# Token routing with a reordered chain to the gather, one-hots built in one operation, and first-layer matmuls of the first expert placed between the count groups of the second round

## The chip, the cores and the metric

The kernel runs on one core of a Trainium2 chip. The metric is the device time of one execution in microseconds (us). An execution that the hardware profiler recorded comes with it: its trace holds each instruction of each engine with start and duration.

## The reference

Three layers follow one another. Sink-and-window attention gives 1536 tokens of 512 values. A greedy mixture of eight experts routes them: all 1536 x 8 scores are taken from the highest down, and a token goes to the expert of the score if the token is still free and the expert has fewer than 192 tokens. A second mixture weights all eight experts by a Sinkhorn iteration.

```
for idx in order:                      # scores from the highest down
    tok, e = idx // E, idx % E
    if assigned[tok] >= 0 or counts[e] >= cap:   # cap = N // E = 192
        continue
    assigned[tok] = e
    counts[e] += 1
for e in range(E):
    mask = assigned == e
    out[mask] = maximum(x[mask] @ w1[e], 0) @ w2[e]
```

The change lies in the greedy mixture.

## The kernel before

The greedy assignment is done in eight rounds (r = 0 to 7, called rounds one to eight here). In each round every free token proposes to its best expert that is left; for each proposal the kernel counts how many better ones its expert has, finds the expert whose 192nd token has the highest score, closes that expert, and gathers its 192 tokens as two tiles of 96. The tokens lie as 12 columns of 128 (n = 12); from round five on they are compacted to 6 columns.

One round goes as follows, by the names in the code.

- `propose`: val and the scores L give prop and the score m of each proposal (DVE). PE turns each column of m into a row over all partitions (tile bc, in two PSUM buffers of four columns), ScalarE copies the rows to `row`.
- `count`: for each column c DVE compares the row with m (tiles gt and g; L607, L608, L610), into GB = 4 buffers. The compare over the columns behind c (L610) reads the whole row. PE multiplies these tiles with prop into cnt: 13 matmuls of eight columns for each c, taken in six groups of two columns (26 matmuls, L616). Round one's counts are made within the attention.
- `route`: from cnt DVE forms sel, red and fin; PE sums red over the partitions (tile sm); the highest threshold names the expert (eh); ft holds each chosen token's slot.
- `place_tokens`: DVE builds one-hots oh of the slots (L667, one operation for each column) and ch, PE multiplies them (L674, the slot product), and DVE gets the token numbers, `at` and, as integers, `ixs`. The gather (POOL, L716) reads ixs. After ixs the expert's number EIX is written, on which SyncE's weight loads wait (`load_w`, four loads of 1 MB). In round one the first of these loads is issued earlier, and the three others by ScalarE's queue, after the last row copy of the next proposal.
- `leave`: the chosen tokens and the closed expert are struck out of val.
- `turn_tokens`: PE transposes the gathered tokens (L752), ScalarE copies them to xe.
- `moe1`: 32 matmuls of the first layer (L768, tile mm from xe and the weights wf, relu to hT) and 32 of the second (L779), each of 192 columns in fp32, two rows in the trace. The transposes of the next expert's tokens stand in the middle of the second layer. Then come two products with the second gate (L790).

The scheduler lays out one order for each engine. The routing has a high priority, and `issue_after` pins single instructions behind others; the matmuls of `moe1` fill what PE has left. Each engine then runs its order strictly in sequence, so an instruction that waits holds up all behind it on that engine. The weights share a pool of WB = 6 buffers of 1 MB: round two's first two loads find two free ones. The gathered tokens (xg), xe and row have one buffer each.

Of the kernel before, what the change touches and what calls it, by code (L numbers as in the profile page):

```python
# [8 lines left out]
F32 = mybir.dt.float32  # L9
# [11 lines left out]
def kernel(  # L21
# [494 lines left out]
    def routing_and_moe1():  # L516
# [55 lines left out]
        def propose():  # L572
# [11 lines left out]
            for c0 in range(0, n, 4):  # L584
                pb = ps.tile([P, 4, P], F32, name="bc", bufs=2)
                c1 = min(n, c0 + 4)
# [6 lines left out]
        def count(n, m, prop, row):  # L593
# [3 lines left out]
            turned = st.pop("turned", None)  # L597
            with nullcontext() if turned is None else tc.issue_after(turned):
                nc.tensor.matmul(cnt.rearrange("p c e -> p (c e)"), zb, zb[:, :n * E], start=True, stop=False,
                                 skip_group_check=True)  # L600
            for c0 in range(0, n, GC):
# [12 lines left out]
                for cc, a, b in reversed(blocks):  # L614
                    with nullcontext() if first is None else tc.issue_after(first.ins):
# [5 lines left out]
        def route(r):  # L621
# [11 lines left out]
            nc.vector.tensor_reduce(red, sel.rearrange("p a c e -> p a e c"), axis=AX.X, op=OP.add)  # L633
# [6 lines left out]
            nc.vector.scalar_tensor_tensor(fin, cnt, float(CAP) - 0.5, prop, op0=OP.is_lt, op1=OP.mult)  # L640
# [13 lines left out]
        def place_tokens(r, ft, t1, eh, code, n):  # L654
# [11 lines left out]
            for c in range(n):  # L666
                nc.vector.tensor_scalar(ohs[:, c], slots, ft[:, 2, c:c + 1], None, op0=OP.is_equal)  # L667
            ch = gp.tile([P, n, 2, 2], BF, name="ch", bufs=OB)
            nc.vector.tensor_mul(ch[:, :, 1], code, ft[:, 1].unsqueeze(2).to_broadcast([P, n, 2]))
            nc.vector.tensor_sub(ch[:, :, 0], code, ch[:, :, 1])  # L670
            first = None
            for c in reversed(range(n)):
                with nullcontext() if first is None else tc.issue_after(first.ins):
                    mm = nc.tensor.matmul(sm[:HC, 0:4], ohs[:, c], ch[:, c].rearrange("p h a -> p (h a)"),  # L674
                                          start=(c == n - 1), stop=(c == 0), skip_group_check=True)
                first = first or mm
# [11 lines left out]
        def leave(ft, eh, n):  # L688

            val = st["val"]  # L690
            nc.vector.tensor_scalar(ft[:, 3], ft[:, 0], 0.5, None, op0=OP.is_gt)
            nc.vector.scalar_tensor_tensor(val, eh.unsqueeze(1).to_broadcast([P, n, E]), -100.0, val, op0=OP.mult,
                                           op1=OP.add)
# [47 lines left out]
        XE = {}  # L741
# [15 lines left out]

        def moe1(r):


            w1, w2 = W.pop(r)
            xe = XE.pop(r)
            hT = mp.tile([P, KF, CAP], F32, name="hT", bufs=1)
            for j0 in range(0, KF, 2):
                ph = pm.tile([P, 2, CAP], F32, name="mm", tag="mm", bufs=3)
# [246 lines left out]
```

## Time and profile before

| | |
|---|---|
| median of 3 runs | 1388.39 us (1387.87 to 1389.94) |
| profiled execution | 1387.89 us, its span 1386.2 us |
| PE busy | 1349.7 us, 97% |
| DVE, ScalarE, POOL busy | 811.0, 458.2, 443.3 us |
| granted PE clock, mean | 0.989 |

Busy times are shares of the span, which is the profiled execution without 1.7 us around it. The granted clock is a share of 2.4 GHz; 0.50 is 1.2 GHz. PE's matmuls overlap, so that the time from the start of one to the start of the next is what one costs. An engine's idle time costs nothing where another engine sets the end.

### The profile page before, as it was taken

Reading aid. Unit: us, or ns where it says so; the run is one execution under the profiler, and the core shown is the slowest. Engines: PE = TensorE matmul, PEld = TensorE weight load, DVE = VectorE, ACT = ScalarE, POOL = GpSimd, SP = SyncE. Lnnn points to the kernel's source line nnn. Section 1 sums busy time; section 2 is a strip of 40 time slices with the busy share of each in tenths; the row PEclk is TensorE's granted clock in tenths of the full one; section 3 lists DMA queues with packets and bytes.
Section 4 is the critical chain, followed back from the end, with each engine's and each line's share of the span. In section 5 each row is a group of like instructions: output and inputs, shape, how many; then the busy total and the mean of one; then the engine's idle time right before and its main releaser. Section 6 shows DMA issues by size and latency. Waiting matters only on the chain.

```text
span 1386.2 us, 20957 instructions
## 1 busy us (share of the span) xinstructions
PE 1349.7 (97%) x8195; PEld 1213.9 (88%) x8195; DVE 811.0 (59%) x1921; ACT 458.2 (33%) x975; POOL 443.3 (32%) x612
## 2 busy tenths in 40 slices
PE   7998699999999999999999999999999999999998
PEld 5767599999988998989999998989998998989987
DVE  6777787850458555555555555555555555555554
ACT  6774121221443333333323333333323333333321
POOL 1247010110543333344333333344333333344203
PEclk9999699999999999999999999999999999999999
DMA  7421345477110001011000011011000001011002
GB/s 161 108 62 40 134 167 203 166 185 254 52 31 31 31 31 46 31 34 43 31 31 31 31 32 45 31 36 41 31 31 31 31 33 44 31 38 39 1 1 91
DMA packets 87227, 87.39 MB, mean 63 GB/s; under 512 B 43864, under 2 KB 60248, under 8 KB 87128
## 3 DMA queue, kind: packets, MB, share of 16 engines
q1 hardware_dynamic: 82056, 73.45, 17.1%
q0 software_dynamic: 2944, 9.44, 2.0%
q10 hardware_dynamic: 2128, 3.16, 0.7%
q8 instruction: 64, 1.05, 0.3%
q14 instruction: 35, 0.29, 0.1%
HBM read 79.75 MB, written 6.30 MB: 62 GB/s over the span
## 4 chain that ended last, share of the span: by engine, by line
PE 92%; DVE 4%; ACT 2%; issue 1%; POOL 1%; DMA 0%; POOLq 0%; SPq 0%; DVEq 0%; ACTq 0%
PE pa L927 37%; PE X L870 19%; PE Z L870 9%; PE mm L768 6%; PE mm L779 6%; PE Y L870 5%; PE S L263 2%; ACT pb L276 1%; PE o L322 1%; PE cnt L616 1%; PE PT L312 1%; PE xr L337 1%; DVE pb L266 1%; PE tr L239 1%; POOL out_dram L940 1%
## 5 line engine op out<-in xcount | busy, mean ns | idle before, releaser
L927 PE MATMUL pa<-w,h 128*128 128x512 f32 x2304 | 548.7, 391 | 0.0
L927 PEld LDWEIGHTS pa<-w,h 128*128 128x128 f32 x2304 | 430.3, 188 | 85.2
L938 DVE SCALAR_TENSOR_TENSOR accs<-pa,Pm,accs 128x512 f32<-128x512 f32 x360 | 269.8, 749 | 133.3 <-PE pa L927 130.9
L509 POOL TENSOR_TENSOR w<-r,w 128x256 fp32r<-128x256 f32 x128 | 90.4, 739 | 365.8 <-ACT w L505 365.8
L878 DVE SCALAR_TENSOR_TENSOR h<-sum,h 128x384 fp32r<-128x384 f32 x192 | 136.4, 711 | 58.1 <-ACT h L877 57.9
L489 POOL TENSOR_TENSOR w1l<-r,w1h 128x256 fp32r<-128x256 f32 x96 | 68.6, 743 | 275.1 <-ACT w1h L487 267.1
L877 ACT ACTIVATE h<-sum 128x384 fp32r<-128x384 f32 x192 | 100.4, 523 | 155.9 <-DVE sum L887 155.9
L489 POOL TENSOR_TENSOR w1l<-S,w1h 128x256 fp32r<-128x256 f32 x128 | 102.7, 832 | 0.0
L877 ACT ACTIVATE h<-X 128x384 fp32r<-128x384 f32 x64 | 31.5, 492 | 213.9 <-PE X L870 213.9
L768 PE MATMUL mm<-xe,wf 128*128 128x192 f32 x512 | 96.1, 337 | 0.0
L887 DVE TENSOR_TENSOR sum<-Z,u 128x384 f32<-128x384 f32 x64 | 35.6, 557 | 96.2 <-ACT u L882 96.2
L779 PE MATMUL mm<-hT,wf 128*128 128x192 f32 x512 | 91.5, 331 | 0.0
L887 DVE TENSOR_TENSOR sum<-Y,p 128x384 f32<-128x384 f32 x64 | 35.6, 557 | 88.8 <-PE Y L870 88.7
L768 PEld LDWEIGHTS mm<-xe,wf 128*128 128x128 f32 x512 | 83.4, 193 | 0.1
L779 PEld LDWEIGHTS mm<-hT,wf 128*128 128x128 f32 x512 | 82.6, 190 | 0.5
L716 POOL DMA_INDIRECT xg<-X,ixs x16 | 16.7, 1041 | 168.6 <-PE mm L752 60.6
L878 DVE SCALAR_TENSOR_TENSOR h<-X,h 128x384 fp32r<-128x384 f32 x64 | 35.6, 557 | 53.8 <-ACT h L877 53.8
L882 ACT ACTIVATE p<-X 128x384 f32<-128x384 f32 x64 | 31.4, 491 | 106.8 <-PE X L870 105.0
L882 ACT ACTIVATE u<-X 128x384 f32<-128x384 f32 x64 | 31.5, 492 | 99.3 <-PE X L870 99.3
L505 ACT ACTIVATE w<-r 128x1024 fp32r<-128x1024 f32 x32 | 34.0, 1062 | 89.4 <-PE pa L927 88.2
L276 ACT ACTIVATE pb<-pb,nb 128x264 f32<-128x264 f32 (+1 forms) x96 | 46.3, 488 | 15.6 <-DVE nb L271 15.6
L770 ACT ACTIVATE hT<-mm 128x384 f32<-128x384 f32 x32 | 15.7, 489 | 78.9 <-PE mm L768 78.9
(282 smaller groups left out, 2303.5 us busy)
## 6 DMA issues: line engine op xcount, KB each, us to landing
r<-in_moe_w_dram SPq DMA_DIRECT2D x64, 512.0 KB, 3.4
wf<-in_moe_w_dram SPq DMA_DIRECT2D x29, 1024.0 KB, 7.0
kn<-in_k_dram SPq DMA_DIRECT2D x12, 256.0 KB, 4.1
qn<-in_q_dram SPq DMA_DIRECT2D x12, 256.0 KB, 3.8
vn<-in_v_dram SPq DMA_DIRECT2D x12, 256.0 KB, 3.6
X<-xs POOLq DMA_DIRECT2D x12, 256.0 KB
wf<-in_moe_w_dram ACTq DMA_DIRECT2D x3, 1024.0 KB, 8.8
xg<-X,ixs POOLq DMA_INDIRECT x16
```

What stands on the lines that cost most here:

```text
L276: inorder(nc.scalar.activation(PB[c][:, h, :w], PB[c][:, h, :w], AF.Exp, bias=NB[c][:, 0, h:h + 1], scale=scale, accum_out=NB[c][:, 2, h:h ...
L489: nc.gpsimd.tensor_sub(w1[1][:, o + j], x[:, j], w1[0][:, o + j].bitcast(F32))
L509: nc.gpsimd.tensor_sub(w2[:, 1, f, d], r2[:, f, d], w2[:, 0, f, d].bitcast(F32))
L768: nc.tensor.matmul(ph[:, j - j0, :], w1[j // JH][:, k, j % JH * P:(j % JH + 1) * P], xe[:, k, :], start=(k == 0), stop=(k == KD - 1))
L779: nc.tensor.matmul(py[:, k - k0, :], w2[j // JH][:, j % JH, k * P:(k + 1) * P], hT[:, j, :], start=(j == 0), stop=(j == KF - 1))
L870: nc.tensor.matmul(acc_, w1[a][:, o, k, :], XO[x][t][b][:, k, :], start=(start and n == 0), stop=(stop and n == 3 * KH - 1), skip_group_ch ...
L877: nc.scalar.activation(t[:, 0], x, AF.Relu)
L878: nc.vector.scalar_tensor_tensor(t[:, 1], x, 0.0, t[:, 0].bitcast(F32), op0=OP.max, op1=OP.subtract)
L882: nc.scalar.activation(t, x, AF.Copy)
L887: nc.vector.tensor_add(t, a, b)
L927: nc.tensor.matmul(pa, HT[u, f, h][:, a, j * P:(j + 1) * P], w2[:, b, f, :], start=(n == 0), stop=(n == 3 * FP - 1))
L938: nc.vector.scalar_tensor_tensor(acc[:, c], pa, pe, acc[:, c], op0=OP.mult, op1=OP.add)
```

## The change

- `propose` takes the first four columns of the row in two copies, one of column 0 alone and one of columns 1 to 3.
- `route` moves the two operations on fin behind the reduction red.
- `place_tokens` builds all one-hots in one operation (three operations of four columns in round one), after ch, and multiplies the columns in order.
- `leave` puts its first two operations behind the one-hots.
- `first_layer` is split out of `moe1`. In round one its first 16 matmuls (EARLY = 4 blocks of 128 hidden values, 4 matmuls each, on the first weight half alone) are made ahead of `count`, which pins each of the later count groups of round two behind one of them. `moe1(0)` does the other 16.

```diff
-            for c0 in range(0, n, 4):
+            for c0, c1 in [(0, 1), (1, 4)] + [(x, min(n, x + 4)) for x in range(4, n, 4)]:
                 pb = ps.tile([P, 4, P], F32, name="bc", bufs=2)
-                c1 = min(n, c0 + 4)
...
+            ahead = early if turned is not None else None
...
-                    with nullcontext() if first is None else tc.issue_after(first.ins):
+                    after = first.ins if first else ahead[2 * c0 // GC - 1] if ahead and c0 else None
+                    with nullcontext() if after is None else tc.issue_after(after):
                         mm = nc.tensor.matmul(cnt[:, cc, :], a, b, start=False, stop=(a is blocks[0][1] and c1 == n),
                                               skip_group_check=True)
...
-            nc.vector.tensor_reduce(red, sel.rearrange("p a c e -> p a e c"), axis=AX.X, op=OP.add)
+            summed = nc.vector.tensor_reduce(red, sel.rearrange("p a c e -> p a e c"), axis=AX.X, op=OP.add)
...
-            nc.vector.scalar_tensor_tensor(fin, cnt, float(CAP) - 0.5, prop, op0=OP.is_lt, op1=OP.mult)
+            with tc.issue_after(summed.ins):
+                nc.vector.scalar_tensor_tensor(fin, cnt, float(CAP) - 0.5, prop, op0=OP.is_lt, op1=OP.mult)
...
-            for c in range(n):
-                nc.vector.tensor_scalar(ohs[:, c], slots, ft[:, 2, c:c + 1], None, op0=OP.is_equal)
...
-            nc.vector.tensor_sub(ch[:, :, 0], code, ch[:, :, 1])
-            first = None
-            for c in reversed(range(n)):
-                with nullcontext() if first is None else tc.issue_after(first.ins):
-                    mm = nc.tensor.matmul(sm[:HC, 0:4], ohs[:, c], ch[:, c].rearrange("p h a -> p (h a)"),
-                                          start=(c == n - 1), stop=(c == 0), skip_group_check=True)
-                first = first or mm
+            halves = nc.vector.tensor_sub(ch[:, :, 0], code, ch[:, :, 1])
+            parts = 3 if r == 0 else 1
+            with tc.issue_after(halves.ins):
+                for a in range(parts):
+                    d = slice(a * n // parts, (a + 1) * n // parts)
+                    w = d.stop - d.start
+                    shown = nc.vector.tensor_tensor(ohs[:, d], slots.unsqueeze(1).to_broadcast([P, w, HC]),
+                                                    ft[:, 2, d].unsqueeze(2).to_broadcast([P, w, HC]), op=OP.is_equal)
+            st["slots"] = shown.ins
+            for c in range(n):
+                mm = nc.tensor.matmul(sm[:HC, 0:4], ohs[:, c], ch[:, c].rearrange("p h a -> p (h a)"),
+                                      start=(c == 0), stop=(c == n - 1), skip_group_check=True)
...
-            nc.vector.tensor_scalar(ft[:, 3], ft[:, 0], 0.5, None, op0=OP.is_gt)
-            nc.vector.scalar_tensor_tensor(val, eh.unsqueeze(1).to_broadcast([P, n, E]), -100.0, val, op0=OP.mult,
-                                           op1=OP.add)
+            with tc.issue_after(st["slots"]):
+                nc.vector.tensor_scalar(ft[:, 3], ft[:, 0], 0.5, None, op0=OP.is_gt)
+                nc.vector.scalar_tensor_tensor(val, eh.unsqueeze(1).to_broadcast([P, n, E]), -100.0, val, op0=OP.mult,
+                                               op1=OP.add)
...
+        EARLY = 4
+
+        def first_layer(r, blocks):
+            w1, xe, hT = W[r][0], XE[r], HT[r]
+            made = []
+            for j0 in blocks:
                 ph = pm.tile([P, 2, CAP], F32, name="mm", tag="mm", bufs=3)
                 for j in (j0, j0 + 1):
                     for k in range(KD):
-                        nc.tensor.matmul(ph[:, j - j0, :], w1[j // JH][:, k, j % JH * P:(j % JH + 1) * P], xe[:, k, :],
-                                         start=(k == 0), stop=(k == KD - 1))
+                        made.append(nc.tensor.matmul(ph[:, j - j0, :], w1[j // JH][:, k, j % JH * P:(j % JH + 1) * P], xe[:, k, :],
+                                         start=(k == 0), stop=(k == KD - 1)).ins)
                 nc.scalar.activation(hT[:, j0:j0 + 2, :], ph, AF.Relu)
+            return made
...
+            if r not in HT:
+                HT[r] = mp.tile([P, KF, CAP], F32, name="hT", bufs=1)
+                first_layer(r, range(0, KF, 2))
+            else:
+                first_layer(r, range(EARLY, KF, 2))
...
                     turn_tokens(0)
+                    HT[0] = mp.tile([P, KF, CAP], F32, name="hT", bufs=1)
+                    early = first_layer(0, range(0, EARLY, 2))
```

How the order of the engines moves is shown at three places; where a line number differs between the two kernels, the tiles are the same.

On DVE, in round one, from the masking of fin with the chosen expert to the slot indices (oh are the one-hots, ch the token codes, val the table of what is left), before:

```order
L649 TENSOR_TENSOR fin<-fin,eh 128x96
L692 SCALAR_TENSOR_TENSOR val<-eh,val 128x96
L651 TENSOR_REDUCE ft<-fin 128x12
L662 TENSOR_SCALAR ft<-ft 128x12
L691 TENSOR_SCALAR ft<-ft 128x12
L663 SCALAR_TENSOR_TENSOR ft<-ft 128x12
L669 TENSOR_TENSOR ch<-code,ft 128x12x2
L694 SCALAR_TENSOR_TENSOR val<-ft,val 128x96
L667 TENSOR_SCALAR oh<-slots,ft 128x96 x12
L670 TENSOR_TENSOR ch<-code,ch 128x12x2
L579 TENSOR_REDUCE mx<-val 128x12
L580 SCALAR_TENSOR_TENSOR prop<-val,mx 128x96
```

and the same stretch of DVE with the change:

```order
L653 TENSOR_TENSOR fin<-fin,eh 128x96
L655 TENSOR_REDUCE ft<-fin 128x12
L666 TENSOR_SCALAR ft<-ft 128x12
L667 SCALAR_TENSOR_TENSOR ft<-ft 128x12
L671 TENSOR_TENSOR ch<-code,ft 128x12x2
L672 TENSOR_TENSOR ch<-code,ch 128x12x2
L679 TENSOR_TENSOR oh<-slots,ft 128x384 x3
L700 TENSOR_SCALAR ft<-ft 128x12
L701 SCALAR_TENSOR_TENSOR val<-eh,val 128x96
L687 TENSOR_REDUCE at<-sm 96x2
L703 SCALAR_TENSOR_TENSOR val<-ft,val 128x96
L688 CAST ixs<-at 96x2
```

The updates of val moved behind the one-hots, and the slot indices (at, ixs) ahead of the next proposal's first operations (mx, prop), which follow them now.

On PE, in round two's count, where the first matmuls of the first layer (mm from xe and wf) stand; before, this is the end of the fourth group (after 104 count rows without a break):

```order
L616 LDWEIGHTS gt
L616 MATMUL cnt<-prop,gt 128x8
L768 MATMUL mm<-xe,wf 128x192 x4
L616 LDWEIGHTS g
L616 MATMUL cnt<-prop,g 128x8
```

With the change two of them stand behind each of the first two groups, and eight more are threaded through the third, at whose end it reads:

```order
L619 LDWEIGHTS g
L619 MATMUL cnt<-prop,g 128x8
L776 MATMUL mm<-xe,wf 128x192
L619 LDWEIGHTS gt
L619 MATMUL cnt<-prop,gt 128x8
L776 MATMUL mm<-xe,wf 128x192 x4
```

Up to the end of the sixth group there were 4 and 6 of these matmuls before; now there are 2, 2, 8, 4 and 7 (groups four and five stand together, ahead of the 7). Four follow the sixth group in both.

On PE again, a round's piece later, at the transposes of the tokens that round two gathers (mm from ident and xg); before, they follow two count groups of round three and matmuls of the second layer (mm from hT and wf):

```order
L616 LDWEIGHTS gt
L616 MATMUL cnt<-prop,gt 128x8
L779 MATMUL mm<-hT,wf 128x192 x5
L752 MATMUL mm<-ident,xg_2530 128x96
L752 MATMUL mm<-ident,xg_2532 128x96
```

and with the change they stand behind the slot product (oh) and the row of m (bc), ahead of all count groups of round three:

```order
L683 MATMUL sm<-ch,oh 96x4
L800 MATMUL mm<-hT,wf 128x192 x4
L589 MATMUL bc<-ident,m 128x128 x4
L800 MATMUL mm<-hT,wf 128x192
L589 MATMUL bc<-ident,m 128x128 x8
L800 MATMUL mm<-hT,wf 128x192 x5
L761 MATMUL mm<-ident,xg_2533 128x96
L761 MATMUL mm<-ident,xg_2535 128x96
```

Between the sixth count group and these transposes stood 38 matmuls of the two layers before, and 25 stand there now; both places have 48 of them behind them in all.

## Rows read from the trace of the kernel before

**Rows 1.** Page: the granted PE clock in 40 slices of the span, in tenths.
```profile
PEclk9999699999999999999999999999999999999999
```

**Rows 2.** Windows: busy us of each engine, granted clock, DMA share, GB/s.
```profile
138.00:161.00 23.00, 10.62 (x150) 9.05 (x151) 18.00 (x65) 2.67 (x5) 2.91 (x5) 0.50 0.51 180
...
167.00:195.00 28.00, 28.00 (x343) 27.11 (x341) 23.15 (x75) 5.95 (x12) 1.83 (x2) 1.00 0.45 166
```

**Rows 3.** Timeline of DVE, rounds one and two: start us, us, instruction.
```profile
144.02 1.94 DVE L667 TENSOR_SCALAR oh<-slots,ft 128x96 bf16<-128x96 bf16 x12
...
147.41 0.16 DVE L680 CAST ixs<-at 96x2 int32<-96x2 f32 x1
...
151.60 2.47 DVE L610 TENSOR_SCALAR g<-row,m 128x1408 bf16<-128x1408 f32 x3
...
160.33 0.34 DVE L607 SCALAR_TENSOR_TENSOR gt<-row,m,before 128x128 bf16<-128x128 f32 x1
...
164.56 1.01 DVE L608 TENSOR_SCALAR g<-row,m 128x1536 bf16<-128x1536 f32 x1
...
174.72 0.15 DVE L680 CAST ixs<-at 96x2 int32<-96x2 f32 x1
...
192.10 0.55 DVE L739 TENSOR_TENSOR xB11l<-yT,xB11h 128x384 fp32r<-128x384 f32 x1
```

**Rows 4.** Timeline of PE, rounds one and two.
```profile
146.08 1.04 PE L674 MATMUL sm<-ch,oh 128*96 128x4 bf16 x12 [4.63 <-DVE ch L670]
...
152.87 1.22 PE L752 MATMUL mm<-ident,xg 96*128 96x96 f32 x6 [0.65 <-DMA xg<-X,ixs]
...
167.51 0.17 PE L616 MATMUL cnt<-prop,gt 128*128 128x8 bf16 x1
...
173.79 0.66 PE L674 MATMUL sm<-ch,oh 128*96 128x4 bf16 x12
...
184.20 0.66 PE L752 MATMUL mm<-ident,xg 96*128 96x96 f32 x6
```

**Rows 5.** Chain that ended last, in order of time: start us, us, what.
```profile
160.47 0.86 PE cnt L616 x26
161.32 2.77 PE mm L768 x8
...
169.57 4.33 PE mm L768 x26
...
175.21 0.87 PE bc L589 x8
...
179.96 0.63 PE cnt L616 x26
```

**Rows 6.** Timeline of ScalarE behind the row copies of round one.
```profile
152.49 1.62 ACTq L709 DMA_DIRECT2D wf<-in_moe_w_dram  x3
154.16 0.87 ACT L754 ACTIVATE xe<-mm 128x384 f32<-128x384 f32 x2 [2.63 <-PE mm L752]
```

**Rows 7.** DMA queues (q1 SyncE, q0 POOL): packets, MB; stretches from 152, 179, 180, 182, 211.
```profile
q0 software_dynamic: 30, 0.06, 15.8%
...
q1 hardware_dynamic: 203, 0.42, 107.0%
...
q0 software_dynamic: 63, 0.20, 48.8%
...
q0 software_dynamic: 46, 0.12, 38.5%
...
q0 software_dynamic: 5, 0.00, 1.8%
```

**Rows 8.** Windows: granted clock, third number from the end, around its changes.
```profile
134.50:136.30 1.80, 0.00 (x0) 0.00 (x0) 1.61 (x6) 0.28 (x1) 1.41 (x2) 1.00 0.39 146
137.90:139.00 1.10, 0.75 (x16) 0.56 (x15) 0.47 (x3) 0.00 (x0) 0.89 (x4) 0.50 0.01 4
...
165.00:166.00 1.00, 1.00 (x7) 1.00 (x7) 0.56 (x1) 0.00 (x0) 0.00 (x0) 0.95 0.00 0
```

More of the change, by code (lines that the diff above doesn't have):

```diff
@@ L739, in operands @@
                 nc.vector.tensor_sub(xl, x, xh.bitcast(F32))
-        XE = {}
+        XE, HT = {}, {}
         def turn_tokens(r):
@@ L756, in turn_tokens @@
                 st["turned"] = turned.ins
[L758 to L764, printed above, removed]
+        EARLY = 4
[3 more added lines that the diff above has]
+            for j0 in blocks:
                 ph = pm.tile([P, 2, CAP], F32, name="mm", tag="mm", bufs=3)
@@ L767, in moe1 @@
                     for k in range(KD):
-                        nc.tensor.matmul(ph[:, j - j0, :], w1[j // JH][:, k, j % JH * P:(j % JH + 1) * P], xe[:, k, :],
-                                         start=(k == 0), stop=(k == KD - 1))
+                        made.append(nc.tensor.matmul(ph[:, j - j0, :], w1[j // JH][:, k, j % JH * P:(j % JH + 1) * P], xe[:, k, :],
+                                         start=(k == 0), stop=(k == KD - 1)).ins)
                 nc.scalar.activation(hT[:, j0:j0 + 2, :], ph, AF.Relu)
+            return made
+        def moe1(r):
+            if r not in HT:
[3 more added lines that the diff above has]
+                first_layer(r, range(EARLY, KF, 2))
+            w2 = W.pop(r)[1]
+            del XE[r]
+            hT = HT.pop(r)
             if r % 2 == 0:
```

## The prediction

> **What bounds the kernel now.** The page's clock line comes first: TensorE (PE) has nine tenths of its full speed or more in 39 of 40 slices, and six tenths in the fifth, 139 to 173 us [rows 1]. The windows put that stretch at 138 to 161 us, where round one's routing runs and round two's counting begins: PE works 10.62 of 23 us, at 1.2 GHz (granted 0.50), while VectorE (DVE) works 18. From 167 us PE is full at 2.4 GHz [rows 2]. So the routing is paid for in two currencies: until about 161 us in latency on DVE, after it in PE work alone, as long as PE never waits. What the change is worth is read at one place: how far PE has come when it must next wait for something.
>
> **What the timelines say.** Round one builds its twelve one-hots in 1.94 us, has its slot indices (ixs) at 147.41, and starts the compares over the whole row at 151.60. The compares of columns 8 to 11 begin at 160.33 and the last ends at 164.56 + 1.01 = 165.57 [rows 3]. PE does four count groups before it takes any first-layer matmul (a pass, below; two rows of the trace); the sixth ends at 167.51 + 0.17 = 167.7 with 10 of the 64 matmuls (of expert one's two layers) done. The slot product of round two stands at 173.79, the transposes of its gathered tokens at 184.20 [rows 4]. The chain gives the prices: one pass costs 2.77/4 = 0.69 us at the half clock and 4.33/13 = 0.333 us at the full one, a count group 0.86 or 0.63, a transpose of a column maximum 0.11 [rows 5].
>
> **Round one's chain.** Small operations issue 1.94/12 = 0.16 us apart [rows 3]. Ahead of the one-hots one of the two fin operations goes (0.16; the second stands behind the threshold's maximum instead) and three updates go (0.5). A 128x384 tensor operation takes 0.55 us [rows 3], so three issue in about 1.5 us: 0.4 saved. The slot product takes 1.04 us for twelve columns [rows 4] and now only its last four (0.35) follow the last one-hot: 0.7 saved. ixs come about 1.8 us earlier, at 145.6. The proposal is then all behind them, where two of its operations had lain under the product, so the maxima m gain 1.1 us; the row copies are four instead of three through two PSUM tiles, which costs 0.4 of that: the compares over the whole row start at 150.9, 0.7 earlier. Dropping the reversed order of the slot products and adding the code of early passes costs no instructions; the matmuls are the same ones.
>
> **The gather of round one** lands earlier too, but this isn't what the first passes wait for. ScalarE issues three weight loads in 152.49 to 154.1 and copies xe right behind, at 154.16 [rows 6]. Those loads hang on the last row copy, so xe moves only 0.7 us: the first pass can start at about 154.0.
>
> **Round two's count, by the order.** From 154.0 PE has two passes (155.4), group two (156.25), two passes (157.6) and 17 rows of group three (158.2), all at the half clock. Before, the clock was back at 165.05 [rows 8], 3.9 us after the unbroken stretch that began with the first matmul at 161.2, or 4.6 us after the group of 160.47 [rows 5]. Here the unbroken stretch begins at 154.0; I take the longer of the two, 158.6. The eight passes threaded through group three end at 161.3. The compares of column 8 write the buffer that column 4's rows read until then (four buffers, GB), so they start at 161.3 and not at 159.6, and the four columns take 165.57 - 160.33 = 5.2 us as before: the last compare ends at 166.5. PE meanwhile does four passes, groups four and five and seven passes to 166.9, and the sixth group ends at **167.6**. That is the old time, with 23 matmuls done instead of 10: 13 x 0.333 = **4.3 us** of PE work is in hand.
>
> **Where it goes.** Behind the sixth group the new order has 25 matmuls (8.3 us), the two small products (0.66 at most each, as the slot product [rows 4]) and the twelve transposes of m (1.3) in front of the token transposes: PE is there at 178.4. Before, 38 matmuls and two count groups of the next round stood there. The tokens aren't there yet. Round two's ixs, 7.2 us behind the sixth group before (174.72 + 0.16 [rows 3]), are now 6.6 us behind it (four matmuls, the product, eleven matmuls, the slot product and 0.6 us), at 174.2. From ixs to the last gathered packet passed 8.1 us in that round: the first 1 MB of expert two's weights was taken first, at 0.42 MB in a microsecond and without one gathered packet in 179 to 180; the gather's own packets came in 180 to 183, the last 46 in the last of these microseconds, and none after 183.0 [rows 7]. Both issues hang on the same two DVE operations, ixs and EIX, which still stand together, so the order is the same. In round one, with the queue free, PE had the last tokens at 152.87 [rows 4], 5.3 us after ixs, with the last 30 packets in 152 to 153 [rows 7]; for the step from the last packet to PE I take 0.4 as an estimate from these two. So the tokens can be used at 174.2 + 8.1 + 0.4 = 182.7, and PE **waits 4.3 us**. Counted in states: before, PE began the transposes at 184.20 with 48 matmuls and two groups of round three done; now it begins them at 182.7 with the same 48 and no group, worth 183.96. **0.2 us** is left of the gain. In the old order the transposes stood 0.8 us behind the tokens; that cover is gone.
>
> The Trainium skill, DMA: Bandwidth & Descriptors, section Queues, rings and completion order, says each DMA engine takes turns between the queues that have work. By that the gather would pass the weights at half rate and the wait would be near that of the third case below; this trace doesn't agree: 203 weight packets and no gathered one in 179 to 180 us [rows 7].
>
> **Two later terms.** In round three the new order has PE at the transposes 8.4 us behind ixs (slot product, four matmuls, the m transposes, nine matmuls, a group, three matmuls, a group, one). There the last gathered packets came after 211 us, 9.1 us behind ixs, and with 0.4 more the wait is 1.1; by the 8.5 of round two it is 0.1. I take **0.6**. Round four's transposes stand behind some 27 matmuls and the later ones a whole round behind, so they wait for nothing. And a pause of PE can cost its clock: in 134.5 to 136.3 PE stood still at a granted 1.00, and from 137.9 on it has 0.50 [rows 8]. A wait of 4.3 us is more than twice that pause, so I expect the fall, and the 3.9 to 4.6 us that the return took at half speed cost 1.95 to 2.3 us if it falls at the wait's end, less if earlier: **1.7**, with 0 and 2.3 as ends. The Trainium skill, TensorE: Matmul & The Clock Gate, section HAM oscillation, describes this pattern, a wait for a DMA between bursts that leaves the next burst cold; the row at 137.9 agrees.
>
> **Sum.** The profiled execution took 1387.89 us, 0.5 below the median of 1388.39. 1387.89 - 0.2 + 0.6 + 1.7 = **1390.0 us**, 0.12% above that median: within the 0.2% (2.8 us: 1385.6 to 1391.2) that a measurement of this kernel can tell from no change. The shorter chains of later rounds give nothing, since PE is the bound there and no wait of it was left to shorten.
>
> **Rivals.**
> - *The wait, but no fall of the clock:* 1387.89 - 0.2 + 0.6 = 1388.3. For it speaks that the fall at 137.9 is the only one that the trace shows and came 1.6 us after the pause's end.
> - *The gather isn't held up:* as in round one, 5.3 us behind ixs, at 179.5. The wait is 1.1, too short for a fall, and 1387.89 - 4.3 - 0.1 + 1.1 = 1384.6. Against it stand rounds two and three, whose gathers both came behind the weights [rows 7].
> - *Slower:* the clock comes back as late as it did before, at 165 (in 138 to 161 PE worked 10.62 us and stayed at 0.50 [rows 2]). Then the eight passes in group three take 5.5 us, group three ends at 164.1, column 8's compares wait for it, the sixth group ends at 170.4, and all behind it moves: 1392.8. It decides against "no change" if the clock is back after 161. Against it, the stretch from 154.0 on has no hole.
> - *The passes don't move:* excluded, the order of PE has them there.
>
> **Chances.** The forecast (wait and fall) 0.50, running from 1388.8 to 1392; no fall 0.22; gather not held up 0.13; late clock 0.15. Faster is the third case and a little of unknown cause, 0.14; slower the fourth and the upper end of the first, 0.28; same 0.58. The range of 1386.3 to 1392.6 leaves out most of the third case and the end of the fourth, and its reach upward is the 2.3 us of the clock and the 1.1 of round three.
>
> **What would show it.** In the changed kernel: ixs of round one near 145.6 and the compares over the whole row near 150.9; first-layer matmuls from 154; the clock at 1.00 by about 159; the sixth group's end near 167.6 with 23 matmuls done; a pause of PE of about 4 us ahead of the token transposes, released by the gather, and a stretch at 0.50 behind it; a second pause under 1.2 us one round later. I am wrong if the gather's packets run among the weights', if the pause is under 2 us, or if the sixth group ends beyond 169.

## The result and the profile after

The changed kernel takes 1399.6 us (median of four runs, 1397.31 to 1401.53) against 1388.34 us before: 1.0074 times as long, 95% interval 1.0062 to 1.0085. It is slower by some 10 to 11 us (by the ratio and by the medians), and the forecast of 1390.0 us and its range to 1392.6 us were wrong. The profiled execution took 1400.6 us, with a span of 1398.9 us.

The page's clock line and its line for TensorE (PE): the clock line has changed by a tenth in one slice [rows 1].

```profile
PE 1360.8 (97%) x8195; PEld 1221.2 (87%) x8195; DVE 813.5 (58%) x1859; ACT 460.4 (33%) x982; POOL 443.2 (32%) x612
...
PEclk9999689999999999999999999999999999999999
```

Forty slices of 35 us are too coarse. The windows of the changed kernel (columns as in [rows 2]) show what they hide:

```profile
138.00:161.00 23.00, 13.71 (x139) 11.25 (x140) 18.70 (x64) 2.83 (x6) 5.39 (x9) 0.57 0.42 144
...
157.00:166.00 9.00, 9.00 (x71) 7.65 (x70) 6.72 (x16) 0.49 (x1) 0.00 (x0) 0.50 0.85 325
166.00:167.00 1.00, 1.00 (x7) 0.83 (x6) 0.09 (x1) 0.00 (x0) 0.00 (x0) 0.62 0.00 0
167.00:195.00 28.00, 23.85 (x254) 22.49 (x254) 19.17 (x54) 5.19 (x11) 1.84 (x2) 0.86 0.47 165
...
189.00:197.00 8.00, 8.00 (x75) 7.66 (x74) 5.46 (x12) 1.39 (x3) 0.00 (x0) 0.50 0.66 256
197.00:198.00 1.00, 1.00 (x9) 0.94 (x9) 0.00 (x0) 0.00 (x0) 0.00 (x0) 0.76 0.00 0
...
235.00:238.00 3.00, 3.00 (x35) 2.83 (x34) 0.02 (x1) 0.00 (x0) 0.00 (x0) 0.51 0.03 5
```

PE is busy for all of 157 to 166 us and stays at 1.2 GHz (granted 0.50) throughout. From 167 to 195 it works 23.85 us of 28 at 0.86, where it was full at 1.00 before. Another stretch at half clock is 189 to 197, and a third, in the middle of unbroken work, 235 to 238.

The timeline of DVE, which carries the routing; the first row is the copy of the counts with which round one begins:

```profile
141.29 0.26 DVE L391 COPY cnt<-cp 128x96 f32<-128x96 f32 x1 [0.63 <-PE cp L389]
...
148.73 0.16 DVE L688 CAST ixs<-at 96x2 int32<-96x2 f32 x1
...
153.58 2.48 DVE L611 TENSOR_SCALAR g<-row,m 128x1408 bf16<-128x1408 f32 x3 [0.41 <-ACT row L590]
...
166.91 0.89 DVE L609 TENSOR_SCALAR g<-row,m 128x1280 bf16<-128x1280 f32 x1 [3.19 <-PE cnt L619]
...
169.05 0.95 DVE L609 TENSOR_SCALAR g<-row,m 128x1408 bf16<-128x1408 f32 x1 [0.72 <-PE cnt L619]
...
179.41 0.16 DVE L688 CAST ixs<-at 96x2 int32<-96x2 f32 x1
```

The same copy in the kernel before:

```profile
138.83 0.26 DVE L391 COPY cnt<-cp 128x96 f32<-128x96 f32 x1 [0.63 <-PE cp L389]
```

All ahead of it is attention code that the change doesn't touch, and here it ran 2.46 us later. In the sixteen profiles of this study the copy stands between 138.8 and 141.3 us, in no relation to the edits. So times of round one and two are compared below from this copy on ("aligned"). Aligned, ixs are at 146.3 instead of 147.4, and the compares over the whole row at 151.1 instead of 151.6 [rows 3]. Later DVE stands still for 3.19 us and again for 0.72 until PE gives back a buffer of its compares.

The timeline of PE:

```profile
156.63 1.65 PE L776 MATMUL mm<-xe,wf 128*128 128x192 f32 x4 [0.44 <-ACT xe L763]
...
160.23 0.51 PE L619 MATMUL cnt<-prop,g 128*128 128x8 bf16 x12
...
165.88 0.99 PE L776 MATMUL mm<-xe,wf 128*128 128x192 f32 x2
...
172.86 0.17 PE L619 MATMUL cnt<-prop,gt 128*128 128x8 bf16 x1
...
182.04 1.79 PE L800 MATMUL mm<-hT,wf 128*128 128x192 f32 x10
...
186.41 0.30 PE L761 MATMUL mm<-ident,xg 96*128 96x96 f32 x1 [2.58 <-DMA xg<-X,ixs]
188.29 1.38 PE L761 MATMUL mm<-ident,xg 96*128 96x96 f32 x7 [1.57 <-DMA xg<-X,ixs]
...
224.26 0.80 PE L761 MATMUL mm<-ident,xg 96*128 96x96 f32 x7 [0.89 <-DMA xg<-X,ixs]
```

The early passes begin at 156.63. The sixth count group ends at 173.03, aligned 2.9 us later than before [rows 4], with 23 passes done instead of 10. At 183.8 PE has nothing left but the second round's token transposes, and waits 2.58 + 1.57 = 4.15 us for the gather; it waited for nothing there before. The clock falls at 187.2, within this wait, and is back at 197.5 (these edges, and those named below, are read from windows of a tenth of a microsecond). One round on PE waits 0.89 us more.

The DMA queues of the changed kernel (as in [rows 7]) from 183, 185 and 187 us on, one microsecond each:

```profile
q1 hardware_dynamic: 199, 0.41, 105.6%
...
q1 hardware_dynamic: 106, 0.20, 66.2%
q0 software_dynamic: 53, 0.15, 37.8%
...
q0 software_dynamic: 37, 0.09, 28.1%
```

In 183 to 184 there are weights alone; from 184 on the gather's packets run beside them, and the last come in 187 to 188, 8.4 us behind ixs. In the kernel before the two queues ran beside each other as well, from 180 to 181 us, right behind the microsecond of weights alone in [rows 7]:

```profile
q1 hardware_dynamic: 117, 0.21, 54.8%
q0 software_dynamic: 63, 0.20, 48.8%
```

### The profile page after: what moved, and what is told of

The parts are those of the page before. It is cut to its first block, busy times and chain, and to the rows that moved or that the text cites. A ratio compares the mean times of both kernels' runs of the same rounds, so it can differ in the third digit from the quotient of the medians.

```text
span 1398.9 us, 20896 instructions
## 1 busy us (share of the span) xinstructions
PE 1360.8 (97%) x8195; PEld 1221.2 (87%) x8195; DVE 813.5 (58%) x1859; ACT 460.4 (33%) x982; POOL 443.2 (32%) x612
## 4 chain that ended last, share of the span: by engine, by line
PE 89%; DVE 4%; ACT 2%; POOL 2%; DMA 2%; issue 1%; ACTq 0%; POOLq 0%; SPq 0%; DVEq 0%
PE pa L950 37%; PE X L893 19%; PE Z L893 9%; PE mm L776 6%; PE mm L800 6%; PE Y L893 5%; PE S L263 2%; DMA xg<-X,ixs 1%; ACT pb L276 1%; PE cnt L619 1%; PE o L322 1%; POOL G L379 1%; PE PT L312 1%; PE tr L239 1%; DVE pb L266 1%
## 5 line engine op out<-in xcount | busy, mean ns | idle before, releaser
L776 PE MATMUL mm<-xe,wf 128*128 128x192 f32 x512 | 100.6, 347 | 0.4 <-ACT xe L763 0.4
L800 PE MATMUL mm<-hT,wf 128*128 128x192 f32 x512 | 97.3, 340 | 0.0
```

The lines of the kernel that those rows point to most:

```text
L776: made.append(nc.tensor.matmul(ph[:, j - j0, :], w1[j // JH][:, k, j % JH * P:(j % JH + 1) * P], xe[:, k, :], start=(k == 0), stop=(k == K ...
L800: nc.tensor.matmul(py[:, k - k0, :], w2[j // JH][:, j % JH, k * P:(k + 1) * P], hT[:, j, :], start=(j == 0), stop=(j == KF - 1))
```

## The experiments

Two theories stood against each other. *The wait*: PE has so little left when the slot list of round two comes that it stands idle until the gather has got through the weight loads, and pays again at half clock behind that. *The late count*: the early passes, at half clock, hold up the count of round two, and all that hangs on it.

The table sets all runs side by side; each ratio is to the kernel before on the same chip (its medians there: 1389.65 us for the first four, 1387.7 for e5 to e8, 1389.3 for e9 to e12, 1389.54 for the last two). "Threshold" is the time from the aligned copy to the first threshold product behind round two's count (before: 168.96 - 138.83; the product stands some 1.3 us behind the sixth group). "Wait" is PE's wait for gathered tokens in round two, "slow" the stretch at 0.50 that begins at its token transposes or just behind them, in us. All three are from the profiled executions, one for each kernel.

```
kernel            median us  ratio, interval         threshold  wait  slow
before            1388.3                                30.1     0     none
after             1399.6     1.0074 1.0062-1.0085       33.0     4.15  187.2-197.5
e1_chain          1390.1     1.0002 0.9993-1.0012       30.6     0     none
e2_early          1400.8     1.0090 1.0073-1.0107       33.1     4.51  186.1-192.9
e3_gather_first   1391.4     1.0007 0.9997-1.0017       32.9     0.70  none
e4_warm           1394.0     1.0040 1.0025-1.0055       32.9     0.28  188.1-191.5
e5_gather_warm    1387.3     0.9987 0.9978-0.9997       30.1     0     none
e6_before_warm    1391.2     1.0022 1.0012-1.0032       32.8     0     none
e7_before_gather  1388.3     1.0004 0.9995-1.0014       29.9     0     none
e8_two_a_group    1393.5     1.0040 1.0026-1.0054       28.6     3.21  183.5-190.3
e9_first_two      1386.6     0.9984 0.9975-0.9994       29.8     0     none
e10_count_clock   1386.0     0.9982 0.9973-0.9992       29.6     0     none
e11_all           1385.7     0.9970 0.9958-0.9983       29.0     0     none
e12_half          1393.4     1.0026 1.0014-1.0039       32.7     3.09  186.4-193.2
e13_clock_only    1392.8     1.0024 1.0014-1.0033       29.6     3.31  183.5-190.3
e14_before_clock  1391.7     1.0011 1.0000-1.0022       31.9     0     none
```

**Which part of the change.** e1_chain is the changed kernel without the early passes:

```diff
-                    HT[0] = mp.tile([P, KF, CAP], F32, name="hT", bufs=1)
-                    early = first_layer(0, range(0, EARLY, 2))
...
-            ahead = early if turned is not None else None
+            ahead = None
```

> The chain part alone (one-hots in one operation, updates later, four row copies), no first-layer matmul between the count groups. Theory (the loss is PE's wait for round two's gather and the slow clock behind it): the order has 14 matmuls, the transposes of m and count groups of round three ahead of the token transposes again, so no wait over 1 us and no fall of the clock after 170 us: 1386 to 1390 us. Rival (the reordered chain itself is what costs): 1395 to 1401 us.

e2_early is the kernel before with first_layer, the early passes and their places in the count, and nothing of the chain.

> The 16 early matmuls alone, the chain as before. Theory: the token transposes of round two stand right behind five second-layer matmuls as in the change, ixs are no earlier, so PE waits 4 to 6 us for the gather, the clock falls behind the wait, and the time is 1397 to 1403 us. Rival (the chain part costs): 1386 to 1390 us.

Measured 1390.1 us, 0.1 above the range of its theory, and 1400.8 us: the shorter chain changes nothing that can be measured, and the early passes are the whole loss. In e1_chain PE comes to the second round's token transposes without a wait, in a row that shows no release:

```profile
187.46 0.86 PE L761 MATMUL mm<-ident,xg 96*128 96x96 f32 x8
```

**The gather's place.** e3_gather_first is the changed kernel with two tiny stores from the gathered tokens on SyncE's queue, ahead of each round's weight loads, which so start only when the tokens have landed:

```diff
                 with tc.issue_after(known.ins):
                     expert()
-                load_w(r, PARTS)
+                landed = [nc.sync.dma_start(seen[a:a + 1, r:r + 1], XG[r][a][0:1, 0:1]).ins for a in range(2)]
+                with tc.issue_after(landed[1]):
+                    load_w(r, PARTS)
```

> The changed kernel with the weight loads of rounds two to eight held on SyncE's queue until the gathered tokens have landed. Theory (the gather stands behind 1 MB of weights): the gather lands about 5.3 us behind ixs instead of 8 to 10, the wait of 4.2 us at the transposes falls to about 1 us, the clock doesn't fall behind it, and the time is 1390 to 1394 us. Rival (the gather is slow by itself, or the wait is only where other lost time shows): 1398 to 1402 us, and the wait stays above 3 us.

e4_warm keeps the gather where the change has it, and puts 36 matmuls that nobody reads (256 columns, into a spare PSUM tile) ahead of the second round's token transposes, in the time in which PE would wait:

```diff
+        def keep_warm(last):
+            pb = ps.tile([P, 4, P], F32, name="bc", bufs=2)
+            with tc.issue_after(last.ins):
+                for _ in range(36):
+                    mm = nc.tensor.matmul(pb[:, :2].rearrange("p a b -> p (a b)"), zb, zw, start=True, stop=True,
+                                          skip_group_check=True)
+            return mm.ins
```

> The changed kernel with 36 matmuls of 256 columns without use (they write a spare PSUM tile) in PE's order where it waits for the gather of round two. The wait stays as long, but PE isn't idle in it. Theory (half of the loss is the clock that falls behind the wait, 9.4 us at half speed, 4.7 us): no stretch at 0.50 behind the wait, 1394 to 1397 us. Rival (the clock would have stayed down anyway, or costs nothing): 1398 to 1402 us.

In e3 the gather has the queues to itself. Packets from 181 and 182 us on, and PE at the transposes:

```profile
q0 software_dynamic: 55, 0.16, 51.0%
...
q0 software_dynamic: 60, 0.20, 67.9%
```

```profile
182.56 0.25 PE L764 MATMUL mm<-ident,xg 96*128 96x96 f32 x1
183.51 0.80 PE L764 MATMUL mm<-ident,xg 96*128 96x96 f32 x7 [0.70 <-DMA xg<-X,ixs]
```

With ixs at 178.5 the gather is through 4.6 us later instead of 8.4, the wait is 0.70 us, the clock stays at 1.00 behind it (it falls once more much later, from 285.1 to 288.5), and of the loss of 0.74% 0.07% are left, although the count is as late as in the changed kernel (32.9). e4 leaves the transposes where they were (their last ends 48.1 us behind the copy, 48.4 in the changed kernel), so the wait is filled and little else: one count group of round three, worth 0.63 us, came into it too. What it wins is 0.34%, or 4.7 us by the ratios. The slow clock accounts for nearly all of that: in the changed kernel 9.2 us behind the wait and 3.4 us at 235 ran at half speed, here 3.4 us did. Its windows over the last useless matmuls with the transposes, and behind them:

```profile
186.00:188.00 2.00, 2.00 (x55) 2.00 (x54) 1.02 (x3) 0.98 (x2) 0.00 (x0) 1.00 1.05 400
188.00:192.00 4.00, 4.00 (x22) 3.94 (x22) 4.00 (x10) 0.00 (x0) 0.00 (x0) 0.57 0.90 349
```

A short stretch at half clock is left, which the theory did not have. The last pause of PE ahead of it is 0.28 us long and lies 2.3 us back.

**The control for the gather.** e7_before_gather is the kernel before with e3's edit.

> The kernel before with the gather of rounds two to eight ahead of their weight loads. Theory (in the kernel before the tokens are there when TensorE comes to them, so nothing is to be won): 1388 to 1391 us, and TensorE waits nowhere for gathered tokens. Rival (the later weights are missed, since 1 MB a round starts later): 1391 to 1396 us, with waits for weights.

Measured 1388.3 us, no change: in the kernel before the gather's place is worth nothing, as PE still has work when the tokens land.

**The idle stretches ahead of the count.** e5_gather_warm is e3 with useless matmuls in two idle stretches, 10 in the tail of the attention part and 18 in round one's `route`; e6_before_warm puts the same into the kernel before. The expectations below place the 18 behind the slot product. In the trace of e5 they run from 140.9 to 145.4, around the threshold product and ahead of the slot product (146.6), so the gaps behind that product stayed as they were:

```diff
+            if r == 0:
+                idle = ps.tile([P, 4, P], F32, name="bc", bufs=2)
+                for _ in range(18):
+                    nc.tensor.matmul(idle[:, :2].rearrange("p a b -> p (a b)"), zb, zw, start=True, stop=True,
+                                     skip_group_check=True)
             fin = rp.tile([P, n, E], F32, name="fin", bufs=2)
```

> The changed kernel with the gather ahead of the weight loads (as in e3_gather_first, 1391.4 us) and 28 useless matmuls of 256 columns, which nobody reads, in TensorE's two idle stretches ahead of round two's count (10 in the tail of the attention part, 18 between round one's slot product and its token transposes). Theory (idle time in front lets the clock fall, and the passes and counts from 156.6 to 166.6 us pay for it): the clock stays up from 138 us on, the sixth count group ends about 4 us earlier: 1384 to 1388 us, faster than before and than the change. Rival (the clock falls in the count whatever precedes it, since its own thin matmuls let it fall): 1389 to 1393 us, as e3_gather_first.

> The kernel before with the same useless matmuls in the same two stretches. Theory: the half clock between 138 and 165 us costs the kernel before some 2 to 4 us of its ten passes and turns: 1384 to 1387 us. Rival: what waits there waits for VectorE and for the first weights, not for TensorE, and a full clock buys nothing: 1388 to 1391 us.

The clock didn't stay up in either. In e5 it fell at 138.2, behind the ten in the attention's tail, so the eighteen useless matmuls themselves ran at half speed; it came back from 145.0 to 148.4 and fell again until 162.1. In e6 it was at half from 137.7 to 168.4. The windows of e5:

```profile
141.00:145.00 4.00, 4.00 (x21) 3.06 (x22) 2.71 (x12) 0.00 (x0) 0.00 (x0) 0.50 0.00 0
150.00:162.00 12.00, 10.80 (x111) 9.36 (x110) 10.96 (x25) 2.83 (x6) 1.25 (x2) 0.50 0.76 268
```

e5 is 0.1% faster than before all the same. The edit also moved the scheduler's order: the single passes are threaded through group four instead of three, and the threshold comes 2.8 us earlier. So e5 doesn't test its theory, although its time lies in the theory's range, and e6 (1391.2 us, 0.22% slower than before) only says that these two places are the wrong ones.

**The count.** e8_two_a_group holds two of the early passes behind each count group:

```diff
                     first = first or mm
+                if ahead:
+                    for x in ahead[c0 + 2:c0 + 4]:
+                        tc.add_manual_dep(x, mm.ins.name, mybir.DependencyInfo(
+                            mybir.DependencyClass.NoSync, mybir.DependencyReason.DATA), reason="two a group")
```

> The changed kernel with two of the early passes held behind each count group, so that no group has eight of them between its blocks (the order is then 2, 2, 4, 6, 6 and 4 passes a group). Theory one (the eight passes in group three at half clock hold up VectorE's buffers, and the rest of the loss is the wait for gathered tokens and the slow clock behind it): the sixth group ends 1 to 3 us earlier, TensorE meets the gather sooner still, and the wait stays: 1394 to 1399 us. Rival (the late count is the whole of the loss): 1388 to 1391 us.

e10_count_clock is e3 with 24 useless matmuls behind round one's token transposes, where PE was partly idle between 153 and 156.6 us:

```diff
+                    idle = pm.tile([P, 2, CAP], F32, name="mm", tag="mm", bufs=3)
+                    with tc.issue_after(st["turned"]):
+                        for _ in range(24):
+                            mm = nc.tensor.matmul(idle.rearrange("p a b -> p (a b)")[:, :256], zb, zw, start=True,
+                                                  stop=True, skip_group_check=True)
-                    early = first_layer(0, range(0, EARLY, 2))
+                    with tc.issue_after(mm.ins):
+                        early = first_layer(0, range(0, EARLY, 2))
```

> The changed kernel with the gather ahead of the weights and 24 useless matmuls of 256 columns behind round one's token transposes, ahead of the first early pass, where TensorE stands idle from 153 to 156.6 us while the tokens are copied. Theory (this idle stretch is what lets the clock fall at 156.5 us, and the half clock up to 166.6 us holds up the passes and the count): granted clock 1.00 from 153 us to the sixth group, which ends about 4 us earlier: 1385 to 1388 us. Rival (it falls in the count whatever stands there, since the count's matmuls are thin): 1390 to 1393 us with half clock somewhere between 156 and 167 us.

e13_clock_only is e10 with the gather behind the weights again, as in the change.

> The changed kernel with the 24 useless matmuls behind round one's token transposes and nothing else, the gather still behind the weights. In e10_count_clock they kept the clock up through the count, with 1386.0 us. Theory (late count and wait for gathered tokens are two losses that add up): the sixth group some 3 us earlier, TensorE still idle for 3 to 5 us at the second round's token transposes and at half clock behind it: 1392 to 1396 us. Rival (with a full clock in the count the gather is through in time): 1385 to 1389 us.

Windows of e10:

```profile
152.00:168.00 16.00, 15.78 (x233) 14.19 (x231) 13.88 (x31) 1.85 (x4) 0.00 (x0) 1.00 0.54 199
168.00:195.00 27.00, 26.91 (x315) 25.97 (x314) 23.33 (x66) 6.21 (x13) 1.84 (x2) 1.00 0.49 171
```

Windows of e13, and its rows of PE at the transposes:

```profile
154.00:181.00 27.00, 26.81 (x312) 24.56 (x310) 23.23 (x63) 4.71 (x11) 1.84 (x2) 1.00 0.46 156
...
185.00:190.00 5.00, 5.00 (x65) 4.83 (x63) 4.34 (x11) 0.98 (x2) 0.00 (x0) 0.50 1.05 406
```

```profile
182.58 0.30 PE L761 MATMUL mm<-ident,xg 96*128 96x96 f32 x1 [1.66 <-DMA xg<-X,ixs]
184.53 0.42 PE L761 MATMUL mm<-ident,xg 96*128 96x96 f32 x1 [1.65 <-DMA xg<-X,ixs]
```

With the idle stretch filled the granted clock is 1.00 through the whole count, the same matmuls included. That isn't so in one profile alone: the mean granted clock of e10's ten executions is 0.992 to 0.994, that of the changed kernel's four 0.984 to 0.989. The threshold comes 3.4 us earlier than in the changed kernel, and with the gather ahead of the weights nothing waits: 1386.0 us, 0.2% faster than before. Without that (e13) 3.31 us of wait and a slow stretch remain, and the kernel is slower than before by 0.24%. e8 gives the same picture by another order: the earliest threshold of all (28.6, 4.4 us earlier than in the changed kernel where 1 to 3 were expected), the wait at 3.21, and 1393.5 us, 0.5 below its range. Its clock came back sooner as well, at 159.6, so order and clock are mixed in it. So both theories hold: a late count and a wait, each worth several us, and each cure leaves the other's loss. (What the late count costs e3 shows only against e10; against the kernel before, e3's 0.07% is within its interval.)

The useless matmuls of e10 and e13 moved the scheduler's order too (two or three passes a group up to group three, the single ones in group four). At the token transposes of e5 and e8 to e13 there are three more matmuls ahead (28 instead of 25), and a count group of round three stands between the second transpose and the third. So the clock and the order aren't told apart by e10 and e13 alone. e5 helps in part: it has e10's passes for each group (2, 2, 3, 9, 4 and 4) at half clock up to 162.1, through the first three groups, and its threshold is only 0.5 us behind e10's. So the half clock up to there costs little. Behind it e5 got its clock back 3.9 us earlier than e3 (aligned), and what that adds to the order isn't told apart. e9_first_two (e3 and e8 together) has e8's order, with less of the clock, and e11_all has all three edits.

> The changed kernel with both cures that helped: the gather ahead of the weight loads (1391.4 us alone) and two early passes held behind each count group (1393.5 us alone). Theory (the wait for gathered tokens and the late count are two separate losses, and behind an earlier count the gather is earlier too): 1386 to 1389 us, the clock back near 160 us, no wait above 1 us for gathered tokens. Rival (both cures remove the same loss, the slow stretch behind the wait): 1390 to 1392 us, as e3_gather_first.

> The three together: gather ahead of the weights, two early passes a count group, and the 24 useless matmuls. Theory: about 1384 to 1387 us, if the clock stays up from 153 us on. Rival (with the count no longer late, TensorE meets the gather again before it has landed, wherever it stands in the queue): a wait of 2 us or more at the second round's token transposes and 1387 to 1391 us.

The windows of e9:

```profile
155.00:161.00 6.00, 6.00 (x66) 5.23 (x65) 6.00 (x14) 0.00 (x0) 0.00 (x0) 0.50 1.04 397
161.00:162.00 1.00, 1.00 (x29) 0.83 (x27) 1.00 (x3) 0.49 (x1) 0.00 (x0) 0.78 0.80 307
162.00:195.00 33.00, 32.86 (x397) 31.84 (x394) 26.91 (x74) 6.70 (x14) 1.83 (x2) 1.00 0.38 142
```

e9 is at half clock for six of the same microseconds and still has its threshold within 0.2 us of e10's, and its median within 0.6. In this order PE never holds up DVE: from 151.2 to 165.1 DVE waits for no buffer, and in e8 it doesn't either, while in the changed kernel it waits 3.9 us and in e10 0.64. What the half clock still costs is PE's own work behind the compares: the threshold of e9 is 1.2 us behind that of e8, which has the same passes for each group and 3.4 us less at half clock. e11 is the fastest, 1385.7 us, 0.30% (0.17 to 0.42%) less than the kernel before; its interval overlaps those of e9 and e10.

**Half the passes, and the kernel before at full clock.** e12_half is the change with EARLY = 2, that is eight early passes.

> The changed kernel with only eight early passes instead of sixteen, weights ahead of the gather as in the change. The kernel before has ten passes done by the end of the count, so theory (the loss comes from TensorE having so little left when the slot list of round two is there) gives a wait for gathered tokens under 3 us: 1388 to 1394 us. Rival (early passes between count groups cost by holding up the count itself, not by what is left behind): 1394 to 1398 us, with the sixth group as late as with sixteen.

e14_before_clock is the kernel before with the 24 useless matmuls of e10.

> The kernel before with the same 24 useless matmuls in the same place. Theory (the early passes are what a full clock in the count is good for, since in the kernel before TensorE waits there for VectorE between groups): 1386 to 1390 us, about the same as before. Rival (the gain of e10_count_clock is the clock's alone, and the early passes bring nothing): 1384.5 to 1386.5 us, as e10_count_clock.

e12 doesn't decide: its 1393.4 us lie in the theory's range, but the wait is 3.09 us, just over its bound, and the threshold is as late as with sixteen passes, as the rival has it. DVE waits only 0.74 us for buffers here; what is late is PE's own work. The clock was back later still, at 169.3:

```profile
156.00:169.00 13.00, 13.00 (x133) 11.82 (x133) 10.72 (x24) 0.53 (x2) 0.00 (x0) 0.50 0.60 230
```

Its ten executions fall into two groups: three took 1389.1 to 1390.0 us at a mean granted clock of 0.990 or 0.991, as long as the kernel before, and seven 1392.9 to 1396.6 us at 0.986 to 0.988. The loss goes with the clock; the profile is of the second group.

e14, at 1391.7 us, is 0.11% above before, with an interval that just reaches no change, and 1.7 us above what the theory allowed. The clock fell twice in its count, the first time at 154.4 amid the useless matmuls, so its rival, full clock without early passes, wasn't put to the test:

```profile
155.00:157.00 2.00, 2.00 (x35) 1.62 (x33) 1.45 (x4) 0.04 (x1) 0.00 (x0) 0.50 1.05 407
...
162.00:168.00 6.00, 6.00 (x50) 5.83 (x48) 4.45 (x10) 0.00 (x0) 0.00 (x0) 0.50 0.08 30
```

## Why the prediction was wrong

- **Round one's chain, right in sign and small.** ixs came 1.1 us earlier (1.8 forecast), the compares over the whole row 0.5 (0.7 forecast). That shortening it brings nothing is shown by e1_chain.
- **The failed step: "the longer of the two, 158.6".** The first pass started where it was put, at 156.63 - 2.46 = 154.2 aligned (154.0 forecast). But the clock, which had come back at 153.1 and fell again at 156.5, returned only at 166.8, aligned 164.3, ten microseconds into unbroken work. One return of the kernel before, counted from two starts (3.9 and 4.6 us), was made a rule there. At half clock the eight passes in group three held back the buffers of DVE's compares for 3.19 us. That is the third rival's path, the late clock (chance 0.15): it put the sixth group at 170.4, and aligned it was at 170.6, beyond the 169 that the prediction named as a sign of being wrong. No run has the change's own order at full clock, so what the clock alone cost there is the rival's own price, 2.8 us, and not a measured one. The runs that have an earlier count, e5 and e8 to e11 and e13, all have another order.
- **The wait, right.** 4.3 us forecast, 4.15 measured, at the place named, with 23 passes done. Both its ends came 3 us later than forecast (aligned 181.4 and 185.8 for 178.4 and 182.7), since both hang on the sixth group: ixs end 6.5 us behind it, 6.6 forecast. What was wrong is the account of the queues: the gather's first packets came only after those microseconds of weights alone, but then ran beside the weights, which the prediction named as a sign of being wrong. The Trainium skill, DMA: Bandwidth & Descriptors, section Queues, rings and completion order, has each engine take turns between queues, and 185 to 186 us, with 53 gathered packets beside 106 of weights, agrees with it; 183 to 184, with 199 and none, doesn't show it. The prediction read the kernel before at 179 to 180 us alone; one microsecond later that trace has both queues too, with 117 packets of weights and 63 gathered ones. e3_gather_first shows the price of the weights ahead, 3.8 us.
- **The slow clock behind the wait, mis-sized.** 1.7 us forecast. From 188.29, where the wait ends, to 197.5 are 9.2 us at half speed, 4.6 us lost. Here too the 3.9 to 4.6 us of that one return [rows 8] were taken for what a return needs. The fall itself was as expected, and e3 and e4 show that it is worth several us: with a wait of 0.70 us there is none, and with the wait filled 3.4 us at half speed are left. The fall from 235.0 to 238.4 costs another 1.7 us, and the sum has no term for it.
- **Round three, right:** 0.89 us against 0.6.

Summed: the forecast of 1390.0, 2.8 more for the late clock (its own rival's price), 2.9 more behind the wait, 1.7 at 235, 0.3 in round three, and 2.46 of the later start in this profile, give 1400.2 us against the 1400.6 that the profiled execution took. The late start is no part of the change. Without it the sum is 9.4 us above the median of before, against 10.3 by the ratio and 11.3 by the medians: 0.9 to 1.9 us stay unexplained.

The late clock's 1392.8 us already stood on top of the wait and of the 1.7 us behind it, and the range ended below it, at 1392.6. What no rival priced are a long return behind the wait (2.9 us more) and a later fall without a wait (1.7). The runs give the interaction: filling the idle stretch alone takes the loss from 0.74 to 0.24% (e13), the gather's place alone to 0.07% (e3), and both turn it into a gain of 0.18% (e10). The one is worth less where the other is made, 0.50 and 0.67% alone and 0.92% together. Why is not shown. The slow stretch behind the wait is 9.2 us long in the changed kernel and 5.8 in e13, but in e2, with the count as late as in the changed kernel, it is 5.1, so an earlier count isn't needed to shorten it. That the early passes, without their costs, are worth something shows in e9 against e7, both with the gather ahead of the weights and neither with a useless matmul: 0.9984 (to 0.9994) with the change, 1.0004 (from 0.9995) without. The two intervals only just miss each other.

## What to carry to other kernels

Work that is moved ahead of a wait gains only if what ends that wait comes earlier too; here the load of the next weights had to go behind the gather, and the count had to come no later, before the early passes paid. Passes threaded between the stages of another engine's chain should be as few per stage as that engine leaves room for: eight inside one group at half clock made DVE wait 3.19 us for a buffer, and with two inside that group (e8, e9) it waited for none. And a forecast of the clock shouldn't make a rule of the one return that a trace shows. It should carry a late return for each pause by itself, and the range should reach to the sum of those that can come together.

## What was not expected of the hardware

- The time that the clock needed to come back under unbroken work wasn't constant: 9.2 us behind the wait of the changed kernel, 5.8 us behind that of e13 (184.5 to 190.3), 5.1 behind that of e2 (187.8 to 192.9), and about 10 in the changed kernel's count (156.6 to 166.8).
- It fell without a pause of PE right ahead of it: at 235.0 us in the changed kernel, at 285.1 in e3, and at 188.1 in e4.
- With 24 useless matmuls in one idle stretch the clock stayed at 1.00 through the count of the changed kernel (e10, e11, e13), but not in the kernel before (e14), and 28 of them in two earlier stretches did not (e5, e6). Each of these is read from one profile.
